# Where the small products of a two-layer attention kernel stand: output pieces of two chunks and one group's query pieces moved beside the values, tile tasks moved with them

## The chip, the cores and the metric

The kernel runs on one core of a Trainium2 chip. A core has five engines with a program each: TensorE (PE, matrix products; PEld are its weight loads), VectorE (DVE), ScalarE (ACT), GpSimd (POOL) and SyncE (SP, which here issues transfers). Each engine works through its program in order and waits for others by semaphores. The metric is the time of the whole program in microseconds (us).

## The reference

What is computed is two equal rounds of attention with one shared key and value head, and of a router that sends two tokens through a gated network:

```python
def _A_ref(x, wq, wk, wv, wo):          # x: 1 x 2048 x 512, 32 heads of 16
    q = (x @ wq) as 32 heads;  k = x @ wk;  v = x @ wv
    p = softmax(q k^T * 16 ** -0.5);  return (p v) @ wo
def _B_ref(x, w_r, w_gate, w_up, w_down):
    r = x @ w_r;  idx = the 2 tokens with the largest r
    y = (silu(x[idx] @ w_gate) * (x[idx] @ w_up)) @ w_down * sigmoid(r[idx])
    return x, with y added at idx
x = x + _A_ref(layernorm(x));  x = x + _B_ref(layernorm(x))
x = x + _A_ref(layernorm(x));  x = x + _B_ref(layernorm(x))
```

## The kernel before

A round of the two is a layer here: layer 1 and layer 2 (`li` 0 and 1 in the code). The 2048 queries are four chunks of 512, the heads four groups of eight, so there are 16 pairs of chunk and group, and each pair is two units. Unit `u` takes 16 steps (`KT`), a layer 512. A step has four score products of 128 keys (L528, PE), four exponentials (L530, ACT), and the value products (L557, PE), which run some steps behind, in runs after every third score product. The unit's values gather in one bank of PSUM, `pO`, in blocks: two of eight steps per unit, but four of four steps in the first and the last unit (`cuts`). Each block fills its part of the bank.

The exponent needs each query's largest score. So the same products are made up to twelve steps earlier (L458, PE), and DVE takes their maxima (L469). At the end of a block's maxima, `max_parts` takes the largest (L488, DVE), and POOL **splits** it into two halves of 16 bits (L493 to L495). This is at steps 16u - 5 and 16u + 3 in units of two blocks: 411, 419, 427, 435 and so on. Two steps later `max_rows` transposes the split on PE (L501), ACT copies it (L503), and SP stores it into the queries, `q_st` (L507), where the scores use it.

All other work is small tasks in between. A task is put into the list of a step by `at(step, ...)`; the list is run after that step's products, in the order in which the entries were made. Those of `max_parts` and `max_rows` are made first, then those of the query pieces and of the divisors (`z_...`), then those of the chunks.

- A **query piece** (`q_piece`) is 16 products of 128 queries for the next pair (L192), a copy by ACT (L349), and two POOL operations (L350, L351); `q_stack` then loads it into `q_st` by SP.
- An **output piece** (`o_piece`) is 16 products (L192) with a quarter of `wo`, a copy by ACT (L687) and an addition on POOL to the tile's residual (L688). A chunk has 16, four for each of its four tiles of 128 tokens.
- A piece can be done **at once** (`whole`): all 16 products together in a bank of the scores, `pS`. Or it stands **beside values** (`put`): four products at a time after a run of value products, in a part of `pO` that the block doesn't use. A block takes two such pieces, one in units of four blocks.
- When a tile's four pieces are added, POOL makes its mean (`mean_pool`, L706 to L720) and, two steps later, its variance (`var_pool`, L725, L706 to L709, L727).
- From `tb` steps after the chunk's end, the **tile tasks** follow, tile by tile, six steps apart: the normalisation (L755), the product with the router's weights (L766), the residual (L778), the router's sum by a tree (L771, L775), all on POOL, and the stores. In layer 1 also the next layer's normalisation (L257 on POOL; for the third chunk L836 on ACT), the turning of the tile (`ln_t`, L262 on PE), and after four tiles keys and values.

What sets the order around the change is a table of step numbers. The steps of the mean are bounded from below for all chunks but the first, to stand behind the tile tasks of the chunk before:

```python
                if n % 4 == 3 and c < NCH - 1:
                    t += 9 * kind + 2
                    if c:
                        t = max(t, 41 + 5 * (n // 4))
```

Here `t` counts from the end of chunk `c`, and `n // 4` is the tile. The buffers that matter are `so0` (outputs, eight), `xh` (three, which normalisations, products and means share), `qf` (two) and the score banks `pS` (three).

Of the kernel before, what the change touches and what calls it, by code (L numbers as in the profile page):

```python
# [9 lines left out]
F32 = mybir.dt.float32  # L10
# [7 lines left out]
P = 128  # L18
S, D, H, DH, F = 2048, 512, 32, 16, 1792
# [9 lines left out]
KT = S // P  # L29
# [15 lines left out]
RUN = 3  # L45
HALVES = 3

T_Q, D_Q, T_ST = 2, 3, (13, 29)
T_Z = 2
MERGE, MERGED_FROM, T_KD = 6, 48, 13  # L50
LOWEST = -3.0e38
# [6 lines left out]
def interleaved_layers(ctx, tc, x_in, wq, wkv, wo, w_r, w_gate, w_up, w_down, out):  # L58
# [354 lines left out]
    def layer(li, src_d, dst_d, early=None):  # L413
# [118 lines left out]
        def pv_mm(hs, halves):  # L532

            t, i = divmod(hs, 2)
            u, r = divmod(t, KT)
            nq = cuts[u]
            b, r = divmod(r, KT // nq)
            w = CW // nq
            nk = nq // 2
            first, last_of = r == 0 and i == 0, r == KT // nq - 1 and i == 1  # L540
            if first and b == 0 and 0 in halves:
                po[u] = psO.tile([P, CW], F32, name="pO")
                so[u] = work.tile([P, CW], F32, name=f"so{u % 2}", bufs=8 - 7 * (u % 2))
            p = pr[hs].rearrange("p h (k j n) -> p h k j n", k=nk, j=2)
            if 1 in halves:
                del pr[hs]

            if nk == 2:
                parts_of = [(k, slice(0, w)) for k in halves]
            elif len(halves) == 2:  # L550
                parts_of = [(0, slice(0, w))]
            else:
                parts_of = [(0, slice(halves[0] * P, (halves[0] + 1) * P))]
            for k, q in parts_of:
                kt = r * nq + i * nk + k
                for j in range(4):
                    nc.tensor.matmul(po[u][32 * j:32 * (j + 1), b * w + q.start:b * w + q.stop],  # L557
                                     v_ext[:, kt, 1 - u % 2:33 - u % 2], p[:, j % 2, k, j // 2, q],
                                     start=kt == 0 and q.start == 0, stop=kt == KT - 1, skip_group_check=True)
            at_block[0] = u, b  # L560
            if last_of and 1 in halves:
                between(u, b, True)
                nc.scalar.copy(so[u][:, b * w:(b + 1) * w], po[u][:, b * w:(b + 1) * w])  # L563
                return True
            return False
# [74 lines left out]
        def z_last(i):  # L640

            u = NU - 1
            w = slice(i * P, (i + 1) * P)
            a, b = so[u - 1][:, w], so[u][:, w]
            pz = bank()[:, :P]
            nc.tensor.matmul(pz, swap[:, 0, :], a, start=True, stop=False)
            nc.tensor.matmul(pz, swap[:, 1, :], b, start=False, stop=True)
            t = work.tile([P, P], F32, name="qf")
            nc.vector.tensor_scalar(t, b, parity[:, 1:2], None, op0=OP.mult)
            if u not in zt:  # L650
                zt[u] = work.tile([P, CW], F32, name="so0", bufs=8)
            o = zt[u][:, w]
            nc.vector.scalar_tensor_tensor(o, a, parity[:, 0:1], t, op0=OP.mult, op1=OP.add)
            nc.vector.reciprocal(t, pz)
            nc.vector.tensor_tensor(o, o, t, op=OP.mult)
            on_last[i] = o
# [189 lines left out]
        for p in range(NCH * NG):  # L846
            e = 32 * p
            if p + 1 < NCH * NG:
                for n in range(4):
                    w = slice(n * P, (n + 1) * P)  # L850
                    if p == 0:
                        at(T_Q + n * D_Q, whole, q_piece, 1, w)
                    else:
                        put(e - 24 + 8 * n, q_piece, p + 1, w)
                for s in range(2):
                    for k in range(NSLOT):
                        at(e + T_ST[s] + k, q_stack, p + 1, s, slice(0, CW), range(2 * k, 2 * k + 2))
                at(e + T_ST[1] + NSLOT, parts.pop, p + 1)
            if p == 0:
                continue  # L860
            c, g = divmod(p - 1, NG)
            u = 2 * p - 1
            at(e + T_Z, z_move, u)
            at(e + T_Z + 2, z_join, u)
            at(e + T_Z + 4, z_recip, u)
            at(e + T_Z + 5, z_store, u)
            at(e + T_Z + 7, z_spread, u, range(2))
            at(e + T_Z + 8, z_spread, u, range(2, 4))
            at(e + T_Z + 10, z_mul, u)
        for c in range(NCH):  # L870
# [1 line left out]
            gs = range(NG)  # L872

            if c < NCH - 2:
                at_once, blocks, tb = (14, 20), range(16, 128, 8), 142
            elif c == NCH - 2:
                at_once, blocks, tb = (14, 21, 28, 35, 42), [*range(16, 72, 8), 72, 72, 80, 80], 98
            else:

                e -= 32 * 2  # L880
                gs = range(2)
                at_once, blocks = (15, 18, 21, 24, 27, 30), [24, 24, 32, 32, 40, 40, 48, 52, 56, 60]
# [40 lines left out]
        def load_wd(n):  # L923
# [5 lines left out]
            else:  # L929
                for k in range(2):  # L930
                    if n == 3:
                        w = work.tile([P, D], F32, name="so0", bufs=8)
                    elif n < 6:
                        w = work.tile([P, D], F32, name=("qh", "ql")[n - 4])
                    else:
# [434 lines left out]
```

## Time and profile before

| | |
|---|---|
| median of three runs | 2678.23 us (2677.62 to 2681.82) |
| the profiled execution | 2678.83 us, its span 2677.1 us |
| mean granted clock of PE | 0.986 of full |
| PE busy | 2615.5 us, 98% |
| DVE busy | 2500.1 us, 93% |
| ACT busy | 2335.1 us, 87% |
| POOL busy | 778.4 us, 29% |

The span is the time from the first to the last instruction; 1.7 us of the execution lie around it. Ends of matrix products are modelled, so a busy PE is not PE at its peak. A step of the stream is found in the trace by its four exponentials: step 0 of layer 1 starts at 56.8 us, that of layer 2 at 1392.5 us, and a step lasts about 2.4 us. A row with an idle time in brackets names what ended it. A product of 32-bit data stands twice in the trace, so 16 products of a piece are x32 there.

### The profile page before, as it was taken

The page shows a single profiled execution, that of the slowest core. Times are in us where ns is not written, and L with a number is a line of the kernel's source. Part 1 is how long each engine was busy: PE and PEld are TensorE (multiplying, and loading weights), DVE is VectorE, ACT ScalarE, POOL GpSimd, SP SyncE. Part 2 cuts the span into 40 slices and gives each one's busy share as a digit, 9 for nine tenths or more (in the row PEclk, how much of TensorE's full clock was granted, in tenths as well). Part 3 has the DMA queues.
Part 4 walks back from the last instruction along what each step waited for, and adds up shares of the span by engine and source line. Part 5 has one row for each costly group of instructions (what it writes and reads, how often), then busy time and mean ns, then how long its engine had stood idle before and what let it go on. Part 6 is the DMA issues. An engine that isn't in the chain of part 4 may idle for free.

```text
span 2677.1 us, 94871 instructions
## 1 busy us (share of the span) xinstructions
PE 2615.5 (98%) x39844; PEld 1266.1 (47%) x39844; DVE 2500.1 (93%) x4499; ACT 2335.1 (87%) x4874; POOL 778.4 (29%) x2100
## 2 busy tenths in 40 slices
PE   7999999999999999999999999999999999999998
PEld 3544444444444444544555444444444444444445
DVE  8999999999999999999679999999999999999995
ACT  2899999999999999898718999999999999999995
POOL 2200001122462126625522000021224522164262
PEclk7999999999999999999979999999999999999999
DMA  3001110000110001011400000000001100010114
GB/s 99 6 23 34 32 58 11 13 12 15 39 38 15 11 13 47 29 31 34 142 15 6 15 15 14 29 11 15 10 15 39 38 12 11 26 34 27 31 52 129
DMA packets 70768, 83.14 MB, mean 31 GB/s; under 512 B 27740, under 2 KB 43676, under 8 KB 70340
## 3 DMA queue, kind: packets, MB, share of 16 engines
q1 hardware_dynamic: 67474, 75.80, 9.3%
q8 instruction: 313, 5.13, 0.8%
q10 hardware_dynamic: 2354, 1.07, 0.1%
q14 instruction: 115, 0.94, 0.1%
q0 software_dynamic: 512, 0.20, 0.0%
HBM read 42.80 MB, written 17.18 MB: 22 GB/s over the span
## 4 chain that ended last, share of the span: by engine, by line
PE 71%; ACT 19%; DMA 3%; issue 2%; POOL 2%; SPq 1%; DVE 1%; ACTq 0%; DVEq 0%; POOLq 0%
PE pO L557 31%; PE pS L528 21%; ACT pr L530 15%; PE pM L458 9%; PE pO L192 5%; DMA q_st<-mr 2%; PE pS L192 2%; ACT wd L462 1%; SPq L507 1%; ACT so L563 1%; ACT qf L687 1%; DMA x<-xl_d,of 1%; DVE mx L469 1%; ACT qf L349 0%; POOL xh L771 0%
## 5 line engine op out<-in xcount | busy, mean ns | idle before, releaser
L469 DVE TENSOR_REDUCE mx<-pM 128x1 f32<-128x512 f32 x3784 | 2318.8, 686 | 93.8 <-PE pM L458 82.4
L530 ACT ACTIVATE pr<-pS 128x512 f32<-128x512 f32 x4044 | 2135.1, 611 | 175.4 <-PE pM L458 132.4
L458 PE MATMUL pM<-k_st,q_st 48*128 48x512 f16 x4096 | 1237.5, 386 | 7.5 <-DVE mx L469 3.8
L528 PE MATMUL pS<-q_st,k_st 50*128 50x512 f16 (+1 forms) x4248 | 1191.4, 371 | 24.4 <-DMA q_st<-mr 6.0
L557 PE MATMUL pO<-pr,v_ext 128*32 128x128 f32 (+1 forms) x22528 | 1176.5, 328 | 6.2 <-ACT so L563 3.2
L557 PEld LDWEIGHTS pO<-pr,v_ext 128*32 128x32 f32 x22528 | 562.9, 109 | 601.0 <-issue 390.3
L528 PEld LDWEIGHTS <-k_st 50*128 50x128 f16 x4352 | 298.9, 95 | 502.4 <-issue 377.7
L458 PEld LDWEIGHTS <-q_st 48*128 48x128 f16 x4096 | 297.2, 94 | 178.4 <-issue 142.0
L493 POOL TENSOR_SCALAR ma<-ma 128x8 f32<-128x8 f32 (+1 forms) x136 | 32.1, 236 | 768.8 <-DVE ma L488 536.6
L688 POOL TENSOR_TENSOR x<-x,qf 128x128 f32<-128x128 f32 x128 | 58.0, 455 | 493.4 <-ACT qf L687 493.2
L192 PE MATMUL pO<-xT,wq_sb 128*32 128x128 f32 x3584 | 180.0, 273 | 0.0
L350 POOL CAST qh<-qf 128x128 f16<-128x128 f32 x120 | 34.8, 290 | 441.7 <-ACT qf L349 441.7
L192 PE MATMUL pO<-wo_sb,so 128*32 128x128 f32 x2816 | 137.0, 273 | 0.0
L192 PEld LDWEIGHTS pO<-xT,wq_sb 128*32 128x32 f32 x3584 | 111.3, 110 | 34.0
L709 POOL TENSOR_TENSOR xh<-xh 128x128 f32<-128x128 f32 (+7 forms) x384 | 97.9, 255 | 30.1
L466 DVE CUSTOM_DVE_ANT_0 wd<-pM,wd 128x512 f32<-128x512 f32 x156 | 106.3, 681 | 0.4 <-PE pM L458 0.4
L192 PEld LDWEIGHTS pO<-wo_sb,so 128*32 128x32 f32 x2816 | 86.6, 110 | 24.0
L462 ACT ACTIVATE wd<-pM 128x512 f32<-128x512 f32 x156 | 95.2, 610 | 0.0
L771 POOL TENSOR_TENSOR xh<-xh 128x256 f32<-128x256 f32 (+8 forms) x216 | 66.5, 308 | 15.0
L563 ACT COPY so<-pO 128x256 f32<-128x256 f32 (+1 forms) x136 | 54.8, 403 | 2.2 <-PE pO L557 2.1
L351 POOL TENSOR_TENSOR ql<-qf,qh 128x128 f16<-128x128 f32 x120 | 51.4, 429 | 9.7
L755 POOL TENSOR_SCALAR xh<-x,mv,rs 128x512 f32<-128x512 f32 x24 | 50.0, 2084 | 0.0
(266 smaller groups left out, 1095.3 us busy)
## 6 DMA issues: line engine op xcount, KB each, us to landing
q_st<-mr SPq DMA_DIRECT2D x512, 1.0 KB
q_st<-qh SPq DMA_DIRECT2D x244, 32.0 KB
zt<-zr_d SPq DMA_DIRECT2D x120, 64.0 KB
xl_d<-xh SPq DMA_DIRECT2D x28, 256.0 KB
pr<-in_w_up SPq DMA_DIRECT2D x12, 448.0 KB
x<-in_x SPq DMA_DIRECT2D x20, 256.0 KB
x_d<-x SPq DMA_DIRECT2D x16, 256.0 KB
x<-x_d SPq DMA_DIRECT2D x16, 256.0 KB
```

Source lines behind the costliest of these rows:

```text
L192: nc.tensor.matmul(out[r], lhsT[:, r], rhs, start=start, stop=stop, skip_group_check=shared)
L458: nc.tensor.matmul(pm, q_st[u][r, j, q:q + P], k_st[r, kc * CW:(kc + 1) * CW], start=True, stop=True)
L462: nc.scalar.activation(rect, pm, AF.Relu)
L466: nc.vector.tensor_tensor_reduce(out=b_over_a, in0=pm, in1=b_over_a, scale=1.0, scalar=LOWEST, op0=OP.add, op1=OP.max, accum_out=mx[u][:, ...
L469: nc.vector.reduce_max(mx[u][:, c, i:i + 1], pm, axis=AX.X)
L528: nc.tensor.matmul(ps[:, k * 2 * w:(k + 1) * 2 * w], k_st[rows, kt * P:(kt + 1) * P], q_st[u][rows, :, b * w:(b + 1) * w], start=True, sto ...
L530: nc.scalar.activation(pr[hs][:, h, :], ps, AF.Exp, scale=DH ** -0.5)
L557: nc.tensor.matmul(po[u][32 * j:32 * (j + 1), b * w + q.start:b * w + q.stop], v_ext[:, kt, 1 - u % 2:33 - u % 2], p[:, j % 2, k, j // 2, ...
L563: nc.scalar.copy(so[u][:, b * w:(b + 1) * w], po[u][:, b * w:(b + 1) * w])
L688: nc.gpsimd.tensor_tensor(x1[i][:, w], x1[i][:, w], y, op=OP.add)
L709: g.tensor_tensor(t[:, :n], t[:, :n], t[:, n:2 * n], op=OP.add)
L771: nc.gpsimd.tensor_tensor(rp_t[i][:, :n], rp_t[i][:, :n], rp_t[i][:, n:2 * n], op=OP.add)
```

## The change

Four edits of the table, and one more buffer of `so0`:

- The 16 output pieces of each of chunks 1 and 2 all stand beside values, at steps 16, 24, ... 136 after the chunk's end. Before, two were done at once (14 and 20) and 14 stood beside values (16 to 120).
- The tile tasks of these two chunks move with them: `tb` is 158 where it was 142, so sixteen steps later. Chunk 2's then run from step 414 on (256 + 158), where it was 398. The bound on the means is not edited.
- The four query pieces of the second pair, done at once at steps 2, 5, 8 and 11, stand beside values in the first unit's four blocks (steps 0, 4, 8, 12). The third pair's first piece, which stood in the third of these, goes to step 16, which then holds two. The second pair's first stack is loaded in two halves, at steps 13 to 15 and 19 to 21.
- The third chunk's tile tasks start one step later, `tb` 99 for 98.

```diff
-T_Q, D_Q, T_ST = 2, 3, (13, 29)
+T_ST = 13, 29
...
-                so[u] = work.tile([P, CW], F32, name=f"so{u % 2}", bufs=8 - 7 * (u % 2))
+                so[u] = work.tile([P, CW], F32, name=f"so{u % 2}", bufs=9 - 8 * (u % 2))
...
-                    if p == 0:
-                        at(T_Q + n * D_Q, whole, q_piece, 1, w)
-                    else:
-                        put(e - 24 + 8 * n, q_piece, p + 1, w)
+                    put(max(e - 24 + 8 * n, KT) if p else KT // cuts[0] * n, q_piece, p + 1, w)
                 for s in range(2):
                     for k in range(NSLOT):
-                        at(e + T_ST[s] + k, q_stack, p + 1, s, slice(0, CW), range(2 * k, 2 * k + 2))
+                        of = range(2 * k, 2 * k + 2)
+                        if p or s:
+                            at(e + T_ST[s] + k, q_stack, p + 1, s, slice(0, CW), of)
+                        else:
+                            at(T_ST[0] + k, q_stack, 1, 0, slice(0, CW // 2), of)
+                            at(T_ST[0] + 6 + k, q_stack, 1, 0, slice(CW // 2, CW), of)
...
             if c < NCH - 2:
-                at_once, blocks, tb = (14, 20), range(16, 128, 8), 142
+                at_once, blocks, tb = (), range(16, 144, 8), 158
             elif c == NCH - 2:
-                at_once, blocks, tb = (14, 21, 28, 35, 42), [*range(16, 72, 8), 72, 72, 80, 80], 98
+                at_once, blocks, tb = (14, 21, 28, 35, 42), [*range(16, 72, 8), 72, 72, 80, 80], 99
```

PE at the start of layer 1's stream, step 2 (L458 are maxima, L557 value products, L192 the query piece, L528 scores):

```order
 L458 MATMUL pM<-k_st,q_st 128x512
 L557 MATMUL pO<-pr,v_ext_118 32x128 x12
-L192 MATMUL pS<-xT,wq_sb 32x128 x16
+L192 MATMUL pO<-xT,wq_sb 32x128 x4
 L528 LDWEIGHTS k_st
 L528 MATMUL pS<-q_st,k_st 128x256
```

The 16 products in a score bank have become four in the bank of the values; the other twelve stand after other runs.

POOL in layer 2, just ahead of the split of step 435 (L709 and L727 end the variance of chunk 3's second tile; L493 to L495 are the split), in the kernel before:

```order
L709 TENSOR_TENSOR xh<-xh 128x2
L709 TENSOR_TENSOR xh<-xh 128x1
L727 TENSOR_SCALAR mv<-xh 128x1
L493 TENSOR_SCALAR ma<-ma 128x8
L494 CAST mp<-ma 128x4x2
```

The same place in the changed kernel (L778 is the residual and L771 the router's tree of chunk 2's last tile):

```order
L727 TENSOR_SCALAR mv<-xh 128x1
L778 TENSOR_TENSOR x_37109<-x_37109,xh 128x512
L771 TENSOR_TENSOR xh<-xh 128x256
L771 TENSOR_TENSOR xh<-xh 128x128
L771 TENSOR_TENSOR xh<-xh 128x64
L771 TENSOR_TENSOR xh<-xh 128x32
L771 TENSOR_TENSOR xh<-xh 128x16
L771 TENSOR_TENSOR xh<-xh 128x8
L771 TENSOR_TENSOR xh<-xh 128x4
L771 TENSOR_TENSOR xh<-xh 128x2
L771 TENSOR_TENSOR xh<-xh 128x1
L493 TENSOR_SCALAR ma<-ma 128x8
```

Residual and tree of a tile have moved in front of the split. Between it and the split of step 427 further up stand, beside what was there, one more residual, one more tree with its copy, and that last tile's normalisation and product; in layer 1 also a normalisation for the next layer (L257).

POOL in layer 1 around the split of step 483 (L755, L766 and L778 are tile tasks of chunk 3's first tile, L688 additions of output pieces), before:

```order
L463 MEMSET mx 128x1
L755 TENSOR_SCALAR xh<-x_18498,mv,rs 128x512
L766 TENSOR_TENSOR xh<-xh,wr_sb 128x512
L688 TENSOR_TENSOR x_22036<-x_22036,qf 128x128
L493 TENSOR_SCALAR ma<-ma 128x8
L494 CAST mp<-ma 128x4x2
L495 TENSOR_TENSOR mp<-ma,mp 128x4x2
L778 TENSOR_TENSOR x_18498<-x_18498,xh 128x512
```

and in the changed kernel:

```order
L463 MEMSET mx 128x1
L688 TENSOR_TENSOR x_22034<-x_22034,qf 128x128
L493 TENSOR_SCALAR ma<-ma 128x8
L494 CAST mp<-ma 128x4x2
L495 TENSOR_TENSOR mp<-ma,mp 128x4x2
L755 TENSOR_SCALAR xh<-x_18454,mv,rs 128x512
L766 TENSOR_TENSOR xh<-xh,wr_sb 128x512
L778 TENSOR_TENSOR x_18454<-x_18454,xh 128x512
```

The normalisation and the product have moved behind the split.

## Rows read from the trace of the kernel before

**Rows 1.** The page's first part: busy us, share of the span and count of each engine.

```profile
PE 2615.5 (98%) x39844; PEld 1266.1 (47%) x39844; DVE 2500.1 (93%) x4499; ACT 2335.1 (87%) x4874; POOL 778.4 (29%) x2100
```

**Rows 2.** A table of stretches: us, then busy us (and count) of PE, PEld, DVE, ACT and POOL, the granted clock (1.00 is full), share and rate of DMA. The first is steps 48 to 127 of layer 1, with query pieces alone; the second steps 160 to 255, with a query piece and an output piece in each block of eight steps.

```profile
184.40:373.40 189.00, 186.36 (x2676) 82.67 (x2678) 186.43 (x334) 177.56 (x365) 16.43 (x65) 1.00 0.11 33
451.50:684.40 232.90, 230.51 (x3598) 108.45 (x3596) 225.31 (x400) 216.16 (x450) 51.34 (x157) 1.00 0.05 13
```

**Rows 3.** Timelines of POOL, PE and ACT in layer 1 around steps 475 to 486: start us, length us, engine, line, operation, tiles, shapes, count, and in brackets the idle time before it and what ended that. The first two rows are the starts of two successive splits of maxima.

```profile
1231.69 0.23 POOL L493 TENSOR_SCALAR ma<-ma 128x8 f32<-128x8 f32 x1 [1.56 <-DVE ma L488]
...
1250.61 2.10 POOL L755 TENSOR_SCALAR xh<-x,mv,rs 128x512 f32<-128x512 f32 x1
...
1254.46 0.23 POOL L493 TENSOR_SCALAR ma<-ma 128x8 f32<-128x8 f32 x1
...
1255.29 0.22 PE L501 MATMUL pM<-ident_h,mp 128*16 128x128 f16 x1 [0.96 <-POOL mp L495]
...
1256.49 0.81 ACT L836 ACTIVATE xh<-x,rs_c,rs 128x512 f32<-128x512 f32 x1 [0.69 <-POOL x L778]
```

**Rows 4.** A table of stretches for the exponentials L530 alone, of which a step has four, so that a stretch of 64 is 16 steps (one more where one reaches over an edge): us of the stretch, busy us (and count) on ACT, granted clock, DMA. Steps 80 to 95, 128 to 143 (with one piece at once), 192 to 207, and 144 to 159 (with one piece at once).

```profile
259.80:297.70 37.90, 33.69 (x65) 1.00 0.10 30
373.40:412.20 38.80, 33.56 (x65) 1.00 0.23 69
529.20:567.80 38.60, 33.62 (x65) 1.00 0.07 19
412.20:451.50 39.30, 33.47 (x64) 1.00 0.03 7
```

**Rows 5.** DVE's timeline at the start of the stream of layer 1 and of layer 2, columns as in rows 3.

```profile
70.65 7.87 DVE L469 TENSOR_REDUCE mx<-pM 128x1 f32<-128x512 f32 x13 [2.11 <-PE pM L458]
...
1405.92 7.87 DVE L469 TENSOR_REDUCE mx<-pM 128x1 f32<-128x512 f32 x13 [1.48 <-PE pM L458]
```

**Rows 6.** The table of rows 4 for steps 480 to 495 of layer 1 and of layer 2, and for steps 486 to 488 of each; and the first 13.0 us of layer 1's stream from the table of rows 2.

```profile
1240.50:1284.80 44.30, 33.26 (x64) 0.92 0.23 73
2568.10:2606.20 38.10, 33.54 (x64) 1.00 0.27 84
...
1257.20:1267.20 10.00, 6.35 (x13) 0.66 0.46 141
2582.40:2589.30 6.90, 6.31 (x13) 1.00 0.30 88
...
56.80:69.80 13.00, 12.96 (x127) 6.99 (x128) 11.24 (x20) 7.11 (x13) 0.61 (x3) 0.50 0.01 1
```

**Rows 7.** POOL's timeline in layer 2, steps 416 to 437, columns as in rows 3. The L493 rows begin the splits of steps 419, 427 and 435.

```profile
2412.88 2.08 POOL L755 TENSOR_SCALAR xh<-x,mv,rs 128x512 f32<-128x512 f32 x1
...
2416.27 1.28 POOL L778 TENSOR_TENSOR x<-x,xh 128x512 f32<-128x512 f32 x1
2417.51 3.40 POOL L771 TENSOR_TENSOR xh<-xh 128x256 f32<-128x256 f32 x9
2420.87 0.25 POOL L493 TENSOR_SCALAR ma<-ma 128x8 f32<-128x8 f32 x1
...
2433.16 0.46 POOL L688 TENSOR_TENSOR x<-x,qf 128x128 f32<-128x128 f32 x1 [8.29 <-ACT qf L687]
2433.58 0.73 POOL L706 TENSOR_TENSOR xh<-x 128x256 f32<-128x256 f32 x1
...
2438.91 0.10 POOL L463 MEMSET mx<- 128x1 f32 x1
...
2441.62 0.25 POOL L493 TENSOR_SCALAR ma<-ma 128x8 f32<-128x8 f32 x1 [1.55 <-PE pM L458]
...
2442.38 1.04 POOL L725 TENSOR_TENSOR xh<-xh 128x512 f32<-128x512 f32 x1
...
2459.57 0.22 POOL L727 TENSOR_SCALAR mv<-xh 128x1 f32<-128x1 f32 x1
2461.61 0.25 POOL L493 TENSOR_SCALAR ma<-ma 128x8 f32<-128x8 f32 x1 [1.83 <-PE pM L458]
```

**Rows 8.** PE's timeline in the same stretch: the transposes L501 that take the splits of steps 427 and 435.

```profile
2445.87 0.22 PE L501 MATMUL pM<-ident_h,mp 128*16 128x128 f16 x1
...
2464.09 0.22 PE L501 MATMUL pM<-ident_h,mp 128*16 128x128 f16 x1
```

**Rows 9.** Layer 1. First POOL and PE in steps 419 to 437: the split of step 419, the output piece of the block at step 416, and the transposes L501 for the splits of steps 427 and 435. Then PE's turning of the last tile of chunk 1 (step 294), POOL's split of step 299, and the output piece of the block at step 296.

```profile
1090.92 0.24 POOL L493 TENSOR_SCALAR ma<-ma 128x8 f32<-128x8 f32 x1
...
1095.73 2.08 POOL L257 TENSOR_SCALAR xh<-x,mv,rs 128x512 f32<-128x512 f32 x1
1104.57 0.46 POOL L688 TENSOR_TENSOR x<-x,qf 128x128 f32<-128x128 f32 x1 [6.76 <-ACT qf L687]
...
1118.24 0.22 PE L501 MATMUL pM<-ident_h,mp 128*16 128x128 f16 x1
...
1136.48 0.22 PE L501 MATMUL pM<-ident_h,mp 128*16 128x128 f16 x1
...
782.81 0.66 PE L262 MATMUL pS<-ident,xh 128*128 128x128 f32 x4
...
796.48 0.25 POOL L493 TENSOR_SCALAR ma<-ma 128x8 f32<-128x8 f32 x1 [1.53 <-DVE ma L488]
...
808.65 0.46 POOL L688 TENSOR_TENSOR x<-x,qf 128x128 f32<-128x128 f32 x1 [4.56 <-ACT qf L687]
```

More of the change, by code (lines that the diff above doesn't have):

```diff
@@ L650, in z_last @@
             if u not in zt:
-                zt[u] = work.tile([P, CW], F32, name="so0", bufs=8)
+                zt[u] = work.tile([P, CW], F32, name="so0", bufs=9)
             o = zt[u][:, w]
@@ L931, in load_wd @@
                     if n == 3:
-                        w = work.tile([P, D], F32, name="so0", bufs=8)
+                        w = work.tile([P, D], F32, name="so0", bufs=9)
                     elif n < 6:
```

## The prediction

> **What bounds the kernel now.** I read the page's busy shares first, then a table of stretches, then the timelines of POOL and PE. PE is busy 98% of the span and POOL 29% [rows 1], which makes POOL look harmless; but a share over the span says nothing about one stretch. The table of stretches splits the steady stream: with query pieces alone, 80 steps take 189.0 us, 2.363 us a step, and DVE is busy 186.4 of them; with an output piece added in every block, 96 steps take 232.9 us, 2.426 a step, and DVE falls to 225.3 while PE stays at 230.5 [rows 2]. So DVE and PE are both within 1 to 3% of full, nothing lost is caught up later, and any wait of PE goes onto the time whole. One such wait stands near the end of layer 1: PE waits 0.96 us at its transpose L501 for the split maxima (L493 to L495), because these stood in POOL's queue behind 22.8 us of other work since the split before [rows 3]. The reader should keep that row in mind: L501 comes two steps after the split in PE's program, and whatever POOL has in front of the split is between them.
>
> **The change part by part.**
>
> Output pieces beside values. In chunks 1 and 2, two pieces each leave "at once" and go into blocks that held one piece; four per layer. What a piece costs at once: 16 steps with one of them take 38.8 us against 37.9 without, and 39.3 against 38.6 in a stretch that also has output pieces (each pair at the same place in the 24-step pattern) [rows 4], so 0.9 and 0.7, mean 0.8. What it costs beside values: 2.426 less 2.363 is 0.063 a step, 0.51 per block of eight [rows 2]. Eight pieces give 8 x 0.8 = 6.4 back and cost 8 x 0.51 = 4.1: a gain of 2.3, between 0 and 3.5.
>
> Second group's query pieces. Four per layer leave steps 2, 5, 8 and 11 for the four quarter blocks. PE's time for the 16 products stays. What can go is DVE's wait: 2.11 us in layer 1 and 1.48 in layer 2 in front of the reduces after the first piece; it then runs 13 reduces through [rows 5]. So the other three are hidden behind DVE already. I take half of 3.59, 1.8, since the first piece's portions still stand in PE's queue. Against it, one piece of the third group moves from step 8 to step 16, into a block with two, at 0.5 per layer. Together a gain of 0.8, between a loss of 1.0 and a gain of 3.6. The split first stack adds six loads of half the width per layer on SP; the second half is loaded at steps 19 to 21 and first read at step 28, seven steps or about 17 us later, so I cost it at nothing; without that cover, its wait would stand in front of one block.
>
> Third chunk one step later. At step 483 of layer 1 the split now stands ahead of the first tile's normalisation (2.1 us) and router product. That removes the 0.96 us wait at L501, the 0.69 of ACT for the tile's residual [rows 3], and what followed: unit 30 of layer 1 takes 44.3 us against 38.1 in layer 2, and in its steps 486 to 488 the clock averages 0.66 of full, 10.0 us against 6.9 [rows 6]. About half of the 6.2 is work that layer 2 doesn't have and stays (normalisation on ACT, turning the tile on PE); I take a gain of 3.0, between 0 and 4.
>
> Tile tasks of chunks 1 and 2 sixteen steps later. This is the part that decides. Those of chunk 2 now begin at step 414 and run to 435, and the means and variances of chunk 3's first two tiles still stand at steps 425 to 432 (the bound "41 + 5" that kept them behind is not moved). Between the split of step 427 and that of step 435, POOL had 18.2 us of work in layer 2, without a pause, from 2441.62 to 2459.79 [rows 7]. Added to it are two residuals (1.24 each, start to start), two router trees (3.36 each), one copy (0.14), and one normalisation with its product (3.39, 2412.88 to 2416.27): 12.7, so 30.9 us. Eight steps last about 20.
>
> When does that queue start? Counted from the split of step 419 (2420.87): the output piece of the block at step 416 frees POOL at 12.7 (2433.16 plus its own time) [rows 7]; before it POOL has some 10 us of the two tasks that now stand there, and its wait for the query piece, so it gets there at about the same point. Then a mean (5.4, 2433.58 to the fill at 2438.91 and its end), a normalisation with product (3.4) and one more add (0.4): the split of step 427 starts at 21.9. PE wants it at 25.0 (2445.87) [rows 8], so no wait there. Then 30.9, then the split's own 0.76: the maxima are ready at 53.6. PE wants them at 43.2 (2464.09) [rows 8]. **Loss in layer 2: 10.4.**
>
> Layer 1 has the same and also the next layer's normalisation on POOL, 2.05 a tile. From 1090.92: that output piece ends at 14.1 (1104.57), then 2.05, 5.4, 3.4, 0.4: 25.3, with the maxima at 26.1 against 27.3 wanted. Then 30.9 + 2.05 + 0.76: 59.0 against 45.6 [rows 9]. **Loss in layer 1: 13.4**, part of it already at step 432, where PE's turning of the third tile (L262) waits for that tile's normalisation. Behind the waiting PE instruction stand all scores and maxima, so ACT and DVE stop too.
>
> Chunk 1's last tile in layer 1 meets chunk 2's first mean at step 307. From the split of step 299 (796.48): the output piece ends at 12.6 (808.65), then normalisation and product 3.4, residual 1.2, tree 3.4, split and copy 0.9, mean 5.4, next normalisation 2.05: 29.0. PE turns that tile at step 310, 16 steps after the turning at 782.81: 16 x 2.43 and some 1 us of other turning put it 25 to 27 after the split [rows 9]. A loss of 2.5, between 0 and 4.
>
> The clock. After each of the two long waits I expect TensorE to be granted 1.2 GHz for a while, as after the much shorter waits at step 485. By [rows 6], those 10.0 us at a mean of 0.66 hold 6.8 at half clock and are 3.1 longer than layer 2's, of which some is turning work: 2.5 per wait, 5.0 in all. Bounds: nothing, and half of the 13.0 us at 0.50 at the start of layer 1 [rows 6], 6.5 each. The Trainium skill, page "TensorE: Matmul & The Clock Gate", section "HAM oscillation — how this bites in real kernels", prices time at the lower clock at half its length; by it the same 6.8 us would be 3.4 per wait, and the sum 1.8 more. The row of this kernel is somewhat below that rule, and I keep the row.
>
> **Sum.** Losses 10.4 + 13.4 + 2.5 + 5.0 = 31.3; gains 2.3 + 0.8 + 3.0 = 6.1; net +25.2. The profiled execution took 2678.83 (span 2677.1 and 1.7 around it), the median of three is 2678.23; from the median, 2703.4, so 2703.
>
> **Rivals.**
>
> The queue clears in time. POOL is not held to the steps; only its order, its data and its buffers hold it. If it got through the 30.9 us ten microseconds sooner (because the gate at 12.7 came earlier, or operations overlapped), PE would meet no wait and only the gains would stand: 2678.2 - 6.1 = 2672. That is the case on the other side; it decides at 43.2 us after the split of step 419 in layer 2. For it speaks POOL's 29%; against it that the operations of [rows 7] run back to back with no room, and that 22.8 us did stop PE at step 485. Chance 0.07.
>
> A wait of a third of the size, 8 us over both layers, without a fall of the clock: 2678.2 + 8 - 6 = 2680, no difference that shows. Chance 0.06.
>
> The waits come, but the clock holds and the turning of tile 3 is covered: 2678.2 + 23.8 - 6.1 = 2696. The chunk's two waits would each have to leave the clock alone, while shorter ones did not. Chance 0.17.
>
> The pieces beside values cost as much as at once, so that part does nothing, and the clock stays low as long as at the start of a layer: 23.8 + 2.5 + 13.0 - 3.8 = 35.5, 2714. Chance 0.10.
>
> The forecast itself: 0.60.
>
> **How the numbers follow.** Low end: queue losses 3 smaller, no clock and no tile-3 loss, all gains at their upper bounds, 11.1: 23.8 - 3 - 11.1 = +9.7, 2688. High end: 23.8 + 4 + 13 - 2 = +38.8, 2717. The cases below 2688 hold 0.13, those beyond 2717 a few hundredths. A run of this kernel is told from no change at about 0.2%, 5.4 us: faster 0.07, same 0.06, slower 0.87.
>
> **What would show it.** In the changed profile: PE idle for about 10 us before L501 at step 437 of both layers, put down to POOL's L495, with POOL busy throughout the 30 us before; a shorter idle before L262 at step 432 of layer 1; clock at half after each. Steps 480 to 495 of layer 1 should be near 41 us with no fall of the clock. Steps 128 to 160 should be near 76.5, not 78.1. The prediction is wrong if POOL's split of step 435 starts less than 25 us after that of step 427, or if PE does other work in front of it.

## The result, and the profile after

The changed kernel takes 2700.43 us (median of six runs, 2697.43 to 2702.15), the kernel before 2680.74 beside it (six runs, 2677.62 to 2682.71): a ratio of 1.0074, 95% interval 1.0061 to 1.0087. It is slower by 19.7 us; forecast were 25, with a range of 10 to 39. The profiled execution has a span of 2696.1 us, 19.0 more than before.

The shares hardly move, as [rows 1] would have it. The first part of the page after:

```profile
PE 2618.0 (97%) x39844; PEld 1265.6 (47%) x39844; DVE 2498.5 (93%) x4499; ACT 2335.3 (87%) x4874; POOL 780.8 (29%) x2100
```

Not even POOL's 29% changes. The next view groups PE's waits: line and tile that waited, the line waited for, us in total, times, the longest.

```profile
PE pM L501 <- POOL mp L495: 15.6, 2, 10.3
...
PE pS L262 <- POOL xh L257: 7.4, 2, 5.3
```

These four waits are 23.0 us, where before L501 waited for POOL for 0.96 at the longest [rows 3]. PE's timeline has them in place: the turning at step 310, the turning at step 432 and the transpose at step 437 of layer 1, and the transpose at step 437 of layer 2.

```profile
819.28 0.65 PE L262 MATMUL pS<-ident,xh 128*128 128x128 f32 x4 [2.13 <-POOL xh L257]
...
1128.82 1.12 PE L262 MATMUL pS<-ident,xh 128*128 128x128 f32 x4 [5.32 <-POOL xh L257]
1148.23 0.27 PE L501 MATMUL pM<-ident_h,mp 128*16 128x128 f16 x1 [5.26 <-POOL mp L495]
...
2482.99 0.27 PE L501 MATMUL pM<-ident_h,mp 128*16 128x128 f16 x1 [10.32 <-POOL mp L495]
```

And POOL's timeline in layer 2 has the queue behind the last of them, cut to its turning points. The L493 rows begin the splits of steps 419, 427 and 435.

```profile
2428.43 0.24 POOL L493 TENSOR_SCALAR ma<-ma 128x8 f32<-128x8 f32 x1 [3.52 <-DVE ma L488]
...
2451.22 0.26 POOL L493 TENSOR_SCALAR ma<-ma 128x8 f32<-128x8 f32 x1
...
2451.99 1.27 POOL L778 TENSOR_TENSOR x<-x,xh 128x512 f32<-128x512 f32 x1
2453.22 1.05 POOL L725 TENSOR_TENSOR xh<-xh 128x512 f32<-128x512 f32 x1
...
2468.89 0.46 POOL L688 TENSOR_TENSOR x<-x,qf 128x128 f32<-128x128 f32 x1
2469.33 2.10 POOL L755 TENSOR_SCALAR xh<-x,mv,rs 128x512 f32<-128x512 f32 x1
...
2477.54 1.27 POOL L778 TENSOR_TENSOR x<-x,xh 128x512 f32<-128x512 f32 x1
2478.76 3.40 POOL L771 TENSOR_TENSOR xh<-xh 128x256 f32<-128x256 f32 x9
2482.13 0.26 POOL L493 TENSOR_SCALAR ma<-ma 128x8 f32<-128x8 f32 x1
```

No row from 2451.22 on has a bracket: POOL never waits, and gets from split to split in 2482.13 - 2451.22 = 30.91 us, where it took 20.0 before [rows 7]. In layer 1 the same pair stands at 1114.35 and 1147.38, 33.03 apart.

The table of stretches (us; busy us and count of PE, PEld, DVE, ACT, POOL; granted clock; DMA) shows the clock: the wait in layer 2, and the rest of the time at half clock behind it.

```profile
2472.70:2483.00 10.30, 0.01 (x1) 0.01 (x1) 0.81 (x2) 0.36 (x2) 8.72 (x26) 0.69 0.10 36
...
2483.00:2486.70 3.70, 3.70 (x33) 1.49 (x35) 1.29 (x2) 2.32 (x5) 0.77 (x4) 0.50 0.02 5
```

The clock is at half from 2476.5 to 2486.8, so 10.2 us; but PE stands still for 6.5 of them. In layer 1 it is at half from 821.1 to 824.5, 1128.3 to 1135.1 and 1145.3 to 1152.2.

The same table for L530 alone (us of the stretch; ACT; clock; DMA) gives the places where time was to come back: steps 0 to 23 of layer 1, 128 to 159, and 480 to 495.

```profile
57.40:126.30 68.90, 51.04 (x97) 0.93 0.02 5
...
373.60:450.10 76.50, 67.21 (x129) 1.00 0.14 39
1258.80:1298.90 40.10, 33.09 (x64) 1.00 0.26 77
```

They are 76.5 for 78.1 with the pieces beside values [rows 4], and 40.1 for 44.3 at the third chunk's tile tasks, whose fall of the clock [rows 6] is gone. From the same exponentials, steps 0 to 23 take 68.9 us where before they took 70.7.

The starts of the exponentials, step for step against the kernel before, say where the 19.0 us lie. Layer 1 loses 5.9 in steps 304 to 320 (2.5 of it the tile tasks' own work, by the version with 57 below, where nothing waits there) and 14.7 in 400 to 448 (16.0 of it in 432 to 440), and gains 4.1 in 480 to 496; layer 2 loses 11.75 in 432 to 440. Steps 128 to 304, where pieces at once are gone, gain 5.1 and 2.8 (in layer 1 partly because tile tasks that stood there now stand behind step 304), and the starts of the layers 1.8 and 0.3.

### The profile page after: what moved, and what is told of

Read it like the earlier page. It is cut to its first block, busy times and chain, and to the rows that moved or that the text cites. A ratio compares the mean times of both kernels' runs of the same rounds, so it can differ in the third digit from the quotient of the medians.

```text
span 2696.1 us, 94892 instructions
## 1 busy us (share of the span) xinstructions
PE 2618.0 (97%) x39844; PEld 1265.6 (47%) x39844; DVE 2498.5 (93%) x4499; ACT 2335.3 (87%) x4874; POOL 780.8 (29%) x2100
## 4 chain that ended last, share of the span: by engine, by line
PE 67%; ACT 18%; POOL 6%; issue 4%; DMA 2%; DVE 2%; SPq 1%; ACTq 0%; DVEq 0%; POOLq 0%
PE pO L557 29%; PE pS L528 20%; ACT pr L530 13%; PE pM L458 9%; PE pO L192 5%; POOL xh L709 2%; ACT wd L462 1%; DMA q_st<-mr 1%; ACT so L563 1%; PE pS L192 1%; SPq L507 1%; ACT qf L687 1%; DVE mx L469 1%; POOL xh L720 1%; DMA x<-xl_d,of 1%
## 5 line engine op out<-in xcount | busy, mean ns | idle before, releaser
L530 ACT ACTIVATE pr<-pS 128x512 f32<-128x512 f32 x4044 | 2134.1, 610 | 187.6 <-PE pM L458 145.7
L458 PE MATMUL pM<-k_st,q_st 48*128 48x512 f16 x4096 | 1236.4, 386 | 7.6 <-DVE mx L469 4.2
L528 PE MATMUL pS<-q_st,k_st 50*128 50x512 f16 (+1 forms) x4248 | 1192.0, 372 | 21.6 <-DMA q_st<-mr 4.9
L557 PE MATMUL pO<-pr,v_ext 128*32 128x128 f32 (+1 forms) x22528 | 1177.3, 328 | 5.4 <-ACT so L563 2.2
L557 PEld LDWEIGHTS pO<-pr,v_ext 128*32 128x32 f32 x22528 | 562.7, 109 | 608.3 <-issue 391.7
L528 PEld LDWEIGHTS <-k_st 50*128 50x128 f16 x4352 | 299.5, 95 | 500.4 <-issue 375.7
L458 PEld LDWEIGHTS <-q_st 48*128 48x128 f16 x4096 | 296.9, 94 | 170.4 <-issue 137.0
L493 POOL TENSOR_SCALAR ma<-ma 128x8 f32<-128x8 f32 (+1 forms) x136 | 32.3, 237 | 781.4 <-DVE ma L488 558.3
L688 POOL TENSOR_TENSOR x<-x,qf 128x128 f32<-128x128 f32 x128 | 58.2, 456 | 481.7 <-ACT qf L687 481.6
L192 PE MATMUL pO<-xT,wq_sb 128*32 128x128 f32 x3840 | 192.5, 273 | 0.0
L192 PE MATMUL pO<-wo_sb,so 128*32 128x128 f32 x3072 | 149.9, 274 | 0.0
L192 PEld LDWEIGHTS pO<-xT,wq_sb 128*32 128x32 f32 x3840 | 119.2, 110 | 34.0
L192 PEld LDWEIGHTS pO<-wo_sb,so 128*32 128x32 f32 x3072 | 94.9, 111 | 26.4 <-issue 0.4
L709 POOL TENSOR_TENSOR xh<-xh 128x128 f32<-128x128 f32 (+7 forms) x384 | 98.5, 257 | 30.1
L771 POOL TENSOR_TENSOR xh<-xh 128x256 f32<-128x256 f32 (+8 forms) x216 | 66.8, 309 | 15.0
L503 ACT CAST mr<-pM 16x128 f16<-16x128 f32 (+1 forms) x136 | 34.3, 252 | 27.7 <-PE pM L501 22.7
```

The source lines that it names most:

```text
L192: nc.tensor.matmul(out[r], lhsT[:, r], rhs, start=start, stop=stop, skip_group_check=shared)
L458: nc.tensor.matmul(pm, q_st[u][r, j, q:q + P], k_st[r, kc * CW:(kc + 1) * CW], start=True, stop=True)
L528: nc.tensor.matmul(ps[:, k * 2 * w:(k + 1) * 2 * w], k_st[rows, kt * P:(kt + 1) * P], q_st[u][rows, :, b * w:(b + 1) * w], start=True, sto ...
L530: nc.scalar.activation(pr[hs][:, h, :], ps, AF.Exp, scale=DH ** -0.5)
L688: nc.gpsimd.tensor_tensor(x1[i][:, w], x1[i][:, w], y, op=OP.add)
L709: g.tensor_tensor(t[:, :n], t[:, :n], t[:, n:2 * n], op=OP.add)
```

## The experiments

The theory was that POOL's order decides: means of chunk 3 and tile tasks of chunk 2 stand in one queue ahead of the split that PE needs. The rivals: pieces beside values or the ninth buffer cost the time; or it is the mere overlap of means and tile tasks, by buffers or contention.

**Move the means behind the tile tasks.**

```diff
-                        t = max(t, 41 + 5 * (n // 4))
+                        t = max(t, 57 + 5 * (n // 4))
```

> The changed kernel with one number edited: the bound on the means is 57 + 5 where it was 41 + 5, so that the means of chunk 3's first two tiles stand at steps 441 and 446, behind chunk 2's tile tasks, and chunk 2's first mean at 313, behind chunk 1's last turning. Theory (POOL's queue ahead of the split of step 435): the queue between the splits of steps 427 and 435 falls from 33.0 and 31.0 us to 18.1 and 16.1, the waits at L501 and L262 go, the falls of the clock with them, and what is left are the gains, which the two traces put at about 10: 2671, between 2668 and 2676. Rival 1 (the fuller blocks, the ninth buffer of so0 or the longer life of the outputs are what costs): no change from the changed kernel, near 2700. Rival 2 (the tile tasks themselves cost more in the later place): between, near 2690.

Measured: 2671.63 us, ratio 0.9972 (0.9961 to 0.9983). In the list of PE's waits no L501 and no L262 waits for POOL any more, and once the clock has risen at the start of a layer's stream, it doesn't fall again up to that stream's end. So one number in a line that the change did not touch takes away the whole loss, with pieces and buffer as they were; and this version is faster than both kernels.

**The tile tasks alone**, on the kernel before, with its pieces and its buffers:

```diff
-                at_once, blocks, tb = (14, 20), range(16, 128, 8), 142
+                at_once, blocks, tb = (14, 20), range(16, 128, 8), 158
```

> The kernel before with one number edited: tb of chunks 1 and 2 is 158 where it was 142, all pieces where they were. Theory: POOL's queue between the splits of steps 427 and 435 is the same 33.0 and 31.0 us as in the changed kernel, so the same waits come (10 us in layer 2, 10 to 11 in layer 1 and the clock behind them, 26 together), chunk 1's last tiles meet the mean at step 297 as well (3 to 6 more), and none of the gains: 2680 + 26 + 5 = 2711, between 2703 and 2716. Rival (the pieces beside values cost it): no loss, 2680.

Measured: 2715.42, ratio 1.0135 (1.0119 to 1.015). Its waits:

```profile
PE pM L501 <- POOL mp L495: 16.6, 4, 9.8
PE pS L262 <- POOL xh L257: 11.0, 2, 5.8
```

The move of the tile tasks costs the time without any of the other edits; the rival of the pieces falls.

**The bound between, 49 for 41** (the line above):

> The changed kernel with the bound at 49 + 5, half way: the means of chunk 3's first two tiles at steps 433 and 438. Theory (a threshold, from the sum of the queue against the 43 to 46 us that PE grants it): layer 2 has 21.4 us between the splits, ready at 42.9 against 43.2, no wait; layer 1 has 23.5, ready at 46 to 47 against 45.6, a wait of 0 to 2; the wait at step 310 of layer 1 stays. So nearly all is back: 2 to 6 us above the kernel with 57, near 2675. Rival (the loss goes with the overlap of means and tile tasks, whatever the moment): half of it stays, 2685 or more.

Measured: 2688.42, ratio 1.0041 (1.0025 to 1.0056): slower than the kernel before. My number missed by 13, and the time is the one that the rival of mere overlap had forecast (2685 or more). L501 still waits twice, 8.0 us in all. POOL's timeline in layer 2, from the split of step 427 to that of step 435, and PE's transpose after it:

```profile
2442.79 0.24 POOL L493 TENSOR_SCALAR ma<-ma 128x8 f32<-128x8 f32 x1 [1.57 <-PE pM L458]
...
2455.22 0.45 POOL L688 TENSOR_TENSOR x<-x,qf 128x128 f32<-128x128 f32 x1 [4.89 <-ACT qf L687]
...
2464.11 1.57 POOL L720 TENSOR_SCALAR xh<-x,mv 128x512 f32<-128x512 f32 x1
2465.65 3.37 POOL L771 TENSOR_TENSOR xh<-xh 128x256 f32<-128x256 f32 x9
2468.99 0.25 POOL L493 TENSOR_SCALAR ma<-ma 128x8 f32<-128x8 f32 x1
...
2469.84 0.27 PE L501 MATMUL pM<-ident_h,mp 128*16 128x128 f16 x1 [4.37 <-POOL mp L495]
```

I had added up POOL's work and left out the bracket: the addition of an output piece, 12 us behind the split, waits 4.89 us for ACT, and everything behind it waits along. Work plus that gate is 26.2 us from split to split, where I had 21.4, and PE comes some 4 earlier. In the changed kernel the same addition (2468.89) finds its data there, since POOL arrives late itself. That repair of the theory had to be tested, with numbers that the rival of mere overlap doesn't give.

**The bound at 51**, which puts the first mean behind the split of step 435 instead of ahead of it:

> The changed kernel with the bound on the means at 51 for 41: the first two means of the next chunk then stand at steps 435 and 440, the first of them just behind the split of step 435 instead of in front of it (with 49 it stood in front). If POOL's order decides, with the waits in its queue counted, both waits at L501 for the split of step 435 go, though means and tile tasks still overlap. In their place: in layer 1 the normalisation of the last tile now stands 8.2 us behind that split instead of directly behind it, so PE should wait some 4.7 us at its turning L262 at step 438; in layer 2 the split of step 443 becomes 0.7 us late; the wait at step 310 (2.1 us, and the fall of the clock after it) stays. Together 8 to 10 over the 2671.6 of the version with 57: 2680 (2677 to 2684). If it were the mere overlap of the means with the tile tasks (buffers, contention) that costs, it stays at the 2688 of the version with 49 or above.

Measured: 2681.74, ratio 1.0004 (0.9995 to 1.0013). Means and tile tasks overlap as with 49, and yet 6.7 us are gone. The expected waits came, if not in the expected sizes; PE's timeline at steps 310 and 438 of layer 1 and 445 of layer 2 (the fill named in the last bracket starts on POOL as the split ends):

```profile
820.05 1.11 PE L262 MATMUL pS<-ident,xh 128*128 128x128 f32 x4 [2.13 <-POOL xh L257]
...
1142.91 0.66 PE L262 MATMUL pS<-ident,xh 128*128 128x128 f32 x4 [2.04 <-POOL xh L257]
...
2489.24 0.22 PE L501 MATMUL pM<-ident_h,mp 128*16 128x128 f16 x1 [1.44 <-POOL mx L463]
```

2.04 for 4.7 at step 438, and 1.44 for 0.7 at step 445; none at step 437. So the order decides; the mere overlap doesn't.

**The gains one by one.** First the third chunk's tile tasks, put back to one step earlier in the version with 57:

```diff
-                ..., [*range(16, 72, 8), 72, 72, 80, 80], 99
+                ..., [*range(16, 72, 8), 72, 72, 80, 80], 98
```

> The kernel with bound 57 and the third chunk's tile tasks back at 98. Theory: POOL has the first tile's normalisation and product ahead of the split of step 483 again, PE waits about 1 us at L501 and ACT for the residual, and the clock falls there in layer 1: 3 to 4 us more than with 99. Rival (the fall of the clock there was chance, and the step later bought nothing): within 1 us of the kernel with 99.

Measured: 2673.64, ratio 0.998 (0.9971 to 0.9989), so 2.0 more than with 99, between the theory's 3 to 4 and the rival's 1; the runs of the two overlap (2669.6 to 2674.3 with 99, 2672.2 to 2676.4 with 98). The wait of 0.96 at L501 is back, as in [rows 3], but not the fall of the clock after it:

```profile
1254.42 0.22 PE L501 MATMUL pM<-ident_h,mp 128*16 128x128 f16 x1 [0.96 <-POOL mp L495]
```

In the table of stretches the 20 us behind it run at a granted clock of 1.00:

```profile
1255.00:1275.00 20.00, 18.25 (x251) 8.65 (x251) 17.32 (x31) 18.67 (x39) 16.94 (x36) 1.00 0.37 111
```

That separates the wait from the clock. The table for L530 alone has steps 480 to 495 of layer 1 in this version, and in the kernel with the query pieces alone (below), where the same wait is followed by a fall of 3.4 us:

```profile
1239.60:1281.70 42.10, 33.36 (x65) 1.00 0.25 77
...
1238.60:1282.20 43.60, 33.28 (x64) 0.96 0.24 74
```

With 99 the same steps take 40.3 by the starts of their exponentials, so the wait and what hangs on it cost 1.8. A fall of 3.4 us adds 1.5, and the fall of 6.8 us in the kernel before (44.3, [rows 6]) 2.2.

Then the query pieces alone, on the kernel before:

```diff
-                    if p == 0:
-                        at(T_Q + n * D_Q, whole, q_piece, 1, w)
-                    else:
-                        put(e - 24 + 8 * n, q_piece, p + 1, w)
+                    put(max(e - 24 + 8 * n, KT) if p else KT // cuts[0] * n, q_piece, p + 1, w)
```

> The kernel before with only the four query pieces of the second group moved beside the values and their first stack loaded in two halves. The prediction gave this part a gain of 0.8 us (between a loss of 1.0 and a gain of 3.6); the trace of the changed kernel, whose two layers reach their steady stream 1.8 and 0.3 us earlier, says about 2.1: 2678 (2676 to 2679.5) beside 2679.8 for the kernel before. If the move does nothing, 2679.8.

Measured: 2677.56 beside 2680.03, ratio 0.9993 (0.9984 to 1.0001): a gain of 1.9 (a loss of 0.3 to a gain of 4.3). The time alone doesn't settle it. In the trace the first 24 steps of the layers gain 1.7 and 0.3, nearly as in the changed kernel, but most of that goes with the moment at which the clock rises (see "The gains" below).

And the output pieces alone, with the tile tasks and the means moved along and the ninth buffer (its lines are as in the change):

```diff
-                at_once, blocks, tb = (14, 20), range(16, 128, 8), 142
+                at_once, blocks, tb = (), range(16, 144, 8), 158
...
-                        t = max(t, 41 + 5 * (n // 4))
+                        t = max(t, 57 + 5 * (n // 4))
```

> The kernel before with the output pieces of chunks 1 and 2 all beside the values, tile tasks sixteen steps later, the ninth buffer, and the bound on the means moved along to 57; the query pieces and the third chunk's tile tasks stay as before. By the prediction's term the pieces gain 2.3 us: 2677.5. By subtraction from the version with all edits and the bound at 57 (2671.6), with 2.1 for the query pieces and 2.0 for the third chunk: 2675.7 (2674 to 2678). If pieces beside values cost as much as at once, 2679.8.

Measured: 2675.17 beside 2680.03, ratio 0.9981 (0.9972 to 0.9989): a gain of 5.1 by the ratio (2.9 to 7.5); its profiled span is 2.8 shorter than before.

**The clock.** Products that nobody reads fill PE's wait at step 437, so that it doesn't stand still. First 40 in layer 2 and 20 in layer 1:

```diff
+        def fill(n):
+            pm = bank()
+            for _ in range(n):
+                nc.tensor.matmul(pm, q_st[27][:KQ, 0, :P], k_st[:KQ, :CW], start=True, stop=True)
+        at(437, fill, 40 if li else 20)
```

> The changed kernel with products that nobody reads put into PE's program just ahead of L501 at step 437, 20 in layer 1 and 40 in layer 2, so that PE works through most of the two waits for the split; the waits themselves stay. It adds work and leaves out nothing. By the prediction each of these waits costs 2.5 us more by the clock that falls after it, so the time should go down by 5.0, to 2695.5. By the trace of the changed kernel (11.75 us lost in layer 2's steps 432 to 440 against a wait of 10.32) the clock's part is 1.4 each: 2697.6 (2696 to 2699). If the clock costs nothing there, 2700.4, and if the products delay L501, more. In the trace the clock should stay at full through 2476 to 2487 us, and no idle time of any length should be left before L501.

Measured: 2702.66, ratio 1.0084 (1.0071 to 1.0097), a miss. Layer 2 in the table of stretches, from the start of the 40 products to the fall, on to their end, and behind them:

```profile
2474.80:2479.10 4.30, 4.30 (x26) 1.90 (x21) 0.96 (x2) 0.51 (x2) 3.67 (x10) 1.00 0.10 34
2479.20:2487.80 8.60, 8.60 (x21) 2.81 (x19) 0.00 (x0) 0.00 (x0) 5.80 (x19) 0.50 0.08 30
2487.90:2492.70 4.80, 4.80 (x38) 1.63 (x37) 1.97 (x4) 3.03 (x7) 0.00 (x0) 0.50 0.00 1
```

The clock fell although PE was busy throughout; with two thirds of that time at half clock the 40 products took 13.1 us and held L501 up themselves. This run says nothing on the clock's price. The next two use larger products, of 128 rows and 32-bit data:

```diff
+        def fill(n):
...
+                nc.tensor.matmul(pm, wq_sb[:, k % NDC, :P], xT[:, k % NDC, :CW], start=True, stop=True)
...
+        at(437, fill, 9 if li else 4)
```

> The changed kernel with products that nobody reads ahead of L501 at step 437 again, but of 128 rows and 512 columns of 32-bit data, four in layer 1 and nine in layer 2, since under the 40 smaller ones the clock fell all the same. It adds work and leaves out nothing. Estimated from L360's 0.27 us for 128 columns, nine take some 9.7 us of the wait of 10.32 and four some 4.3 of 5.26. If the clock now stays at full, the time shows its price: by the prediction 2.5 us for each wait, 2695.5; by the trace of the changed kernel 1.4 in layer 2 and about as much in layer 1, 2697.6 (2696 to 2699). If the clock falls during these products as well, it is not PE's idle time as such that makes it fall, and the time stays at 2700 to 2703.

Measured: 2698.88, ratio 1.0074 (1.006 to 1.0088). The time doesn't resolve it from the changed kernel's, but the trace does. In layer 2 the clock stays at full, with POOL as late as ever:

```profile
2474.00:2484.30 10.30, 8.04 (x24) 3.34 (x18) 0.95 (x2) 0.51 (x2) 8.72 (x26) 1.00 0.11 40
```

L501 starts at 2484.33 behind a rest of the wait of 2.29, and steps 432 to 440 are 1.44 us shorter than in the changed kernel, in layer 1 1.52. Last, all four waits filled (two products at step 310, five at 432, seven and nine at 437):

```diff
+        at(437, fill, 9 if li else 7)
+        if li == 0:
+            at(310, fill, 2)
+            at(432, fill, 5)
```

> The same products in front of every long wait of the changed kernel: nine in layer 2, and in layer 1 two at step 310 and five at step 432, both ahead of the turning L262, and seven at step 437. It adds work and leaves out nothing. If the clock stays at full in all of them: step 310's fall gives back some 1.2 us, those after step 437 1.4 each, and the one after step 432 nothing, because POOL's queue is the limit from there to step 437 and the wait at L501 grows from 5.26 to about 8 by what PE gains: 2696.4 (2695 to 2698). If PE's lower clock and not POOL's queue sets the pace between steps 432 and 437, the wait stays at 5.3 and the time falls by 2 to 3 more, to 2694.

Measured: 2697.36, ratio 1.0068 (1.0054 to 1.0081). The clock stays at full up to 1148.5, falls there for 3.4 us, and stays at full in layer 2. POOL's timeline has its two splits in layer 1:

```profile
1113.00 0.25 POOL L493 TENSOR_SCALAR ma<-ma 128x8 f32<-128x8 f32 x1
...
1146.06 0.25 POOL L493 TENSOR_SCALAR ma<-ma 128x8 f32<-128x8 f32 x1
```

The table of stretches has PE between its turning and the products of step 437, and those products up to L501:

```profile
1127.40:1139.00 11.60, 11.39 (x176) 5.49 (x176) 10.23 (x18) 9.66 (x19) 10.54 (x19) 1.00 0.07 24
1139.00:1146.90 7.90, 6.29 (x18) 2.58 (x14) 0.92 (x2) 0.48 (x2) 6.48 (x23) 1.00 0.09 33
```

POOL needs 33.06 us from split to split, with PE at full clock as with PE at half (33.03). PE gains 2.6 us between its turning and L501 (11.5 for 14.15 in the changed kernel), and all of it goes into the wait there, 7.9 for 5.26. So in layer 1 the fall behind step 432 costs nothing: the queue hides it. Against the changed kernel, steps 304 to 312 gain 1.0, steps 432 to 440 of layer 1 0.2, those of layer 2 1.3.

## Why the prediction was right

Its mechanism held: two families of tasks on POOL that the bound "41 + 5" should have kept apart stand in one queue in front of a split. One of its signs came otherwise: in layer 1 the idle time at L501 was 5.26 us and not about 10, since that at L262 before it was not the shorter one but 5.32. The terms against what was measured:

| term | forecast, us | measured, us | read from |
|---|---|---|---|
| layer 2, split of step 435 | 10.4 | 10.32 | the wait at L501 |
| layer 1, the same, with L262 at step 432 | 13.4 | 13.2 | 5.32 + 5.26, and the 2.6 that PE lost at half clock between them |
| turning at step 310 | 2.5 | 2.1 | the wait at L262 |
| the clock | 5.0 | 4.0 | 1.44 and 1.52 (products of 128 rows), 1.0 (step 310) |
| output pieces | -2.3 | -5.1 (-2.9 to -7.5) | that part alone; its profile says -2.8 |
| query pieces | -0.8 | -1.9 (+0.3 to -4.3) | that part alone |
| third chunk | -3.0 | -2.0 to -4.1 | put back; steps 480 to 495 of the changed kernel |

The losses come to 29.6 where 31.3 were forecast. The net is 19.7, so the gains are 9.9, where 6.1 were forecast. The parts measured one by one give 9.0 to 11.1, and the version with 57, in which the gains stand alone, is 8.2 below the kernel before (7.5 by the ratio, 4.6 to 10.5).

**The queue.** The forecast added 12.7 us of moved operations, by their rows, to the 18.2 that stood between the splits, 30.9; the trace has 30.91. The splits of step 427 were to start 21.9 and 25.3 after those of step 419; they start 22.8 and 25.75 after them. Counted from the split of step 419, both ends of layer 2's wait came 1.0 later than forecast (54.6 for 53.6, and 44.2 for 43.2), so this drops out of the 10.32. The addition worked because there POOL had no wait left in its queue. The forecast had not asked for one between the two splits, and in that it was lucky: with the bound at 49 the same addition gave 21.4 us where 26.2 came. The rival that the queue clears in time rested on the earlier gate, the output piece 12.7 us behind the split of step 419; that gate was hardly the limit here, since in layer 2 POOL was still at work when the piece was there, and in layer 1 it waited 0.9 us for it.

**Layer 1.** Its 13.4 was the right total, but it doesn't stand as one wait: part falls at the turning of step 432, part at L501, and the low clock between the two lies inside the total, since POOL goes on meanwhile. A price for the clock on top of each wait counts that stretch twice; here one fall was paid after L501 and one was free.

**The clock.** It was the term that was too large for each wait: 2.5 forecast, 1.4 to 1.5 measured. So the time came out between the forecast and the rival in which the clock holds and the turning of step 310 is covered, 2696. The row behind the 2.5 was read rightly: without its fall the same steps take 2.2 less. But that fall of 6.8 us came after the wait, and PE worked through 6.2 of it. The fall in layer 2 begins inside the wait, and what counts is the low clock while PE works: 3.8 of 10.2 us (2482.99 to 2486.8), and half of 3.8 is 1.9. The Trainium skill, page "TensorE: Matmul & The Clock Gate", section "HAM oscillation — how this bites in real kernels", takes half of the throttled time as the price. An estimate by it from the whole 10.2 us is 5.1, which the runs don't show. Of the fall behind step 310 the prediction had nothing; it cost 1.0.

**The gains.** Together they were taken too small, but not each is shown to be. The query pieces: half of DVE's first wait [rows 5] was a guess, and the interval of that part alone (a loss of 0.3 to a gain of 4.3) holds the forecast's 0.8. The 1.8 at the start of layer 1 doesn't measure it, since these steps take longer the later the clock rises: in the nine profiles with the pieces moved it rises 9.3 to 12.4 us after step 0, and the first 24 steps take 68.8 to 70.3; in the three without, 11.6 to 13.6, and 70.0 to 71.0. With the rise at 11.4 to 11.6 they take 69.8 with the move and 70.0 without, so some 0.2 is left beside the clock. Whether the move also makes the clock rise earlier, these profiles don't settle. The third chunk: the fall of the clock was taken as part of that wait's price, but with the means behind the tile tasks the same wait of 0.96 came without it. The wait's 1.8 is that edit's gain; the fall's 2.2 is so at most in part. The output pieces' prices by [rows 2, 4] were about right where the trace shows them singly: 0.92 and 0.84 back for the two of a chunk (forecast 0.8), 0.4 for each that joins a block (0.5). That part's 5.1 and the 2.8 of its profile differ mostly by the executions that were profiled: that of the kernel before lies 1.2 below the median of its 29 runs (2678.83 for 2680.03), that of the pieces alone 0.9 above the median of its 12 (2676.06 for 2675.17).

**What stays open.** Why a wait of about 1 us at step 485 is followed by a fall of the clock in four kernels and not in the one with 57 and 98. How much the query pieces gain. And the version with 51 is 10.1 slower than that with 57: step for step the two profiles differ by 4.4 at steps 304 to 320, 3.5 at 400 to 448 and 1.5 at 440 to 448 of layer 2, 9.5 in all. The three waits are 5.6 of this. The rest lies where the clock is at half behind the two turnings (6.8 us from 819.6 and 3.4 us from 1143.9), but no run took it away there.

## What to carry to other kernels

When tasks are moved on an engine that works in order, add up its queue between two operations that others wait for, with the rows' durations and with every wait that stands in it, and compare with when the other engine comes; the engine's share over the span says nothing. A bound that keeps two families of tasks apart must move with the family it was written for: here one number, 57 for 41, makes 20 us lost into 8 gained. And time at a low clock costs only where the engine would otherwise have been the limit.

## What the runs showed of the hardware

PE being busy did not hold its clock. With 40 products of 48 rows ahead of L501 it fell to 1.2 GHz after 4.3 us of them and stayed there for 13.7 us; with nine of 128 rows and 32-bit data in the same place it stayed at 2.4 GHz. Which property of these products matters was not tried.

A wait of 0.96 to 1.04 us at the same transpose, at step 485 of layer 1, was followed by half clock in four of five kernels: 2.3 us later in the kernel before and 2.7 in the one with the output pieces alone, for 6.8 us each; 4.3 later with the query pieces alone and 4.2 with the tile tasks alone, for 3.4 us each. In the version with 57 and 98 the clock stayed at full. Steps 480 to 495 took 44.4 and 44.6 us, 43.7 and 43.6, and 42.1.
